# Stores of the weights' float32 words moved from SyncE's queue to GpSimd's, from the fifth block on

## The chip, the cores and the metric

The kernel runs on one core of a Trainium2 chip. The metric is the device time of one execution in microseconds (us). In the rows and in the text PE is TensorE, DVE is VectorE, ACT is ScalarE, POOL is GpSimd and SP is SyncE. SPq and POOLq are the instruction queues of SP and POOL, where DMAs are issued.

## The reference

Causal attention over 4 batches and 12 heads, then two dense layers with a gate from a short convolution, then a layer that rotates by an angle, mixes tokens and adds a dense layer. The inputs are float64; the kernel reads their bits and turns them into float32 itself.

```python
# attention: batch 4, heads 12, seq 448, head_dim 64  ->  x of (4, 448, 768)
attn = softmax(causal(q @ k.T / 8));  x = attn @ v
# dense 1: conv_w (5, 768), w_val and w_out (768, 768)
gate = sigmoid(sum_k conv_w[k] * shifted(x, k))
x = (gate * (x @ w_val)) @ w_out
# dense 2: w_theta, w_ch (768, 768), w_tok_r, w_tok_i (448, 448)
theta = x @ w_theta
y = w_tok_r @ (x * cos(theta)) + w_tok_i @ (x * sin(theta))
u = x + y
out = u + max(u @ w_ch, 0)
```

## The kernel before

Two streams are interleaved. `attention()` is a generator that does one head in five steps. `dense(b)` is a generator for the dense layers of one batch. The attention of batch b+1 is issued between the steps of `dense(b)`, at a pace set by the table `RATE`. A scheduler then fixes the order of each engine's instructions; the written order only guides it.

The weights come as four matrices of six blocks of 128 output columns: n = 0 to 5 is w_val, 6 to 11 is w_out, 12 to 17 is w_theta, 18 to 23 is w_ch. Each block has two halves, g = 0 and 1, of 384 rows. In the first batch a half goes through these steps:

- `load_w` (L202): SP issues the load of the float64 bits, 384 KB, into a tile `cv_raw`.
- `stage_w`, through `to_f32` (L156 to L163): three DVE instructions and one of ACT (L162) make float32 words of it, in place. L163 is the last.
- `split_w` (L221): for w_val and w_out, SP issues a store of these words, 192 KB, from `cv_raw` to a scratch tensor `plain` in HBM. Later batches load the words from there.
- `split_w` again: `pool_hi` (L107, POOL) rounds the words to the matmul's format, into a tile `w_hl`; `pool_lo` (L110, POOL) or `dve_lo` (L113, DVE) writes the remainder.
- `gemm` (L532): nine PE matmuls with the half.

`cv_raw` and `w_hl` share one pool of eight buffers, the tag `wb`. A load can start when the buffer that it gets is free: when POOL has read the old words and their store has landed, or when PE has used the old `w_hl`.

SP issues every DMA of the kernel, in order: loads of q, k, v and weights, the stores, the outputs. POOL issues none. Besides the weights, POOL computes the low parts of activations (`act_lo`, `x_lo`), a part of the convolution (`gate`, L480) and some copies of k (`kk`, L107).

Three more names: `rb` are the reciprocal row sums of the softmax, fetched by SP from a scratch tensor (L451); `z` are the angle's cosine and sine parts (L587 to L603, on ACT, DVE and POOL); L613 are PE's transposes of z, which the token mixing (L627) needs.

Of the kernel before, what the change touches and what calls it, by code (L numbers as in the profile page):

```python
# [33 lines left out]
AHEAD = 2  # L34
# [17 lines left out]
def kernel(  # L52
# [14 lines left out]
    nc = tc.nc  # L67
# [31 lines left out]
    def f32(ap):  # L99
        return ap.bitcast(F32)  # L100
# [5 lines left out]
    def pool_hi(dst, src):  # L106
        nc.gpsimd.tensor_scalar(out=dst, in0=src, scalar1=1.0, scalar2=0.0, op0=ALU.mult, op1=ALU.add)  # L107
# [82 lines left out]
    plain = dram.tile([NW, 2, P, KH * P], F32, name="plain")  # L190
# [3 lines left out]
    def words(t):  # L194
        return t.rearrange("p n two -> p (n two)")[:, 0:CV]
# [18 lines left out]
    def split_w(n, g):  # L214
        if (n, g) not in bits:
            return
        flat = words(bits.pop((n, g))).bitcast(F32)
        t = flat.rearrange("p (c n) -> p c n", n=P)
        kept = n % NW // KC in PLAIN
        if B > 1 and kept and n < NW:  # L220
            nc.sync.dma_start(out=plain[n, g], in_=flat)  # L221
        store = B > 1 and (kept and B > 2 if n >= NW else not kept)
        if n < AHEAD:
            hi, lo = (
                pool.tile([P, S], F32R, tag=tag, name="w_ahead", bufs=12)[:, : KH * P].rearrange("p (c n) -> p c n", n=P)
                for tag in ("act_hi", "act_lo")
            )
        else:
            hl = pool.tile([P, 2, KH, P], F32R, tag="wb", name="w_hl", bufs=8)
            hi, lo = hl[:, 0], hl[:, 1]  # L230
        if n < NW:
            pool_hi(hi, t)
        else:
            nc.scalar.copy(hi, t)  # L234
        (dve_lo if n < NW and int(W_DVE[n // KC]) > g else pool_lo)(lo, t, hi)
        if store and n < AHEAD:
            for a, x in enumerate((hi, lo)):
                nc.sync.dma_start(
                    out=scratch[n, g][:, a * KH * P : (a + 1) * KH * P], in_=f32(x.rearrange("p c n -> p (c n)"))
                )  # L240
        elif store:
            nc.sync.dma_start(out=scratch[n % NW, g], in_=f32(hl.rearrange("p a c n -> p (a c n)")))
        splits[n, g] = (hi, lo)
# [275 lines left out]
    def gemm(acts):  # L519
        n = wn[0]  # L520
        wn[0] += 1
        pt = psum("mm")
        for g in range(2):
            split_w(n + 1, g)
            stage_w(n + 2, g)
            load_w(n + 3, g)
            fetch_w(n + 3, g)
            whi, wlo = splits.pop((n, g))
            for kc in range(g * KH, (g + 1) * KH):
                xhi, xlo = acts[kc]  # L530
                for m, (a, x) in enumerate(((whi, xhi), (whi, xlo), (wlo, xhi))):
                    nc.tensor.matmul(  # L532
                        pt[:, :S], lhsT=a[:, kc % KH, :], rhs=x,
                        start=kc == 0 and m == 0, stop=kc == KC - 1 and m == 2,
                    )
            if g == 0:
                yield
        return pt
# [189 lines left out]
    for n in range(5 * (H + 1) + X_SEG + 1):  # L728
        next(at, None)
        if n == 5:  # L730
            setup_conv()
        if W_AT <= n < 5 * H:
            with tc.issue_after(ttr_ins[-1].ins):
                for at_n, (m, g) in zip(A_TILES, ((0, 0), (1, 0), (0, 1), (1, 1), (2, 0), (2, 1), (3, 0), (3, 1))):
                    if n == at_n - W_AT:
                        load_w(m, g)
                    if n == at_n:
                        stage_w(m, g)
                        if m < AHEAD + 1:
                            split_w(m, g)  # L740
        i, c = divmod(n, 5)
        if AHEAD and i >= 3 and i % 2 == 1 and c == A_SEG:
            gemm_ahead((i - 3) // 2)
        if n == 5 * H - 3:
            with tc.issue_after(ttr_ins[-1].ins):
                for g in range(2):
                    load_w(AHEAD + 2, g)
# [47 lines left out]
```

## Time and profile before

| | before |
|---|---|
| median of 3 runs (lowest to highest) | 778.81 us (778.42 to 780.77) |
| profiled execution, its own time | 784.47 us |
| its span, first to last instruction | 782.4 us |
| PE, DVE, ACT, POOL busy | 714.7, 463.3, 445.0, 331.9 us |
| stores to `plain` from SP | 24, of 192 KB |

The profiled execution has 2.07 us outside its span and is 5.66 us (0.7%) above the median. The shares of busy time are means over stages with different limits: the first batch's dense layers, about 100 to 260 us, are the only stage in which weights are converted and stored to `plain`.

### The profile page before, as it was taken

To read this page: it belongs to the slowest core of one execution; us is meant where nothing else is said; L and a number is where in the kernel's file an instruction comes from. 1 tells how busy PE (TensorE), PEld (TensorE's weight loads), DVE (VectorE), ACT (ScalarE), POOL (GpSimd) and SP (SyncE) were. 2 spreads that over 40 slices of the span, in tenths; PEclk is the share of its full clock that TensorE was granted. 3 is DMA by queue.
4 is the path that set the end of the run, shared out by engine and by line. 5 is a ranking of instruction groups with operands and counts; after the bars stand their busy time and mean duration, and the time that the engine had idled before them with its cause. 6 is when DMAs were issued, how large, how long until landed. Compare 5 with 4: busy or idle time off the path is not lost.

```text
span 782.4 us, 12216 instructions
## 1 busy us (share of the span) xinstructions
PE 714.7 (91%) x4009; PEld 607.5 (78%) x4009; DVE 463.3 (59%) x1104; ACT 445.0 (57%) x1047; POOL 331.9 (42%) x363
## 2 busy tenths in 40 slices
PE   5898978994988998999899999999899998999997
PEld 4665666783867886888688798898788887898996
DVE  4888599887777564463575564564576432115531
ACT  4787665876797454565877344354878331125401
POOL 0597774975476566774164410033062241201100
PEclk9999889998999999899999999999999999999999
DMA  9845337988684398799843288688532187774223
GB/s 227 181 122 146 78 106 224 208 265 187 193 143 123 103 208 279 233 224 338 152 75 99 54 171 232 193 141 240 143 61 66 52 135 233 203 220 139 84 71 81
DMA packets 152940, 125.78 MB, mean 161 GB/s; under 512 B 92815, under 2 KB 130477, under 8 KB 152877
## 3 DMA queue, kind: packets, MB, share of 16 engines
q1 hardware_dynamic: 152877, 125.00, 62.9%
q8 instruction: 32, 0.52, 0.3%
q14 instruction: 31, 0.25, 0.1%
HBM read 95.81 MB, written 29.16 MB: 160 GB/s over the span
## 4 chain that ended last, share of the span: by engine, by line
PE 58%; DVE 15%; ACT 10%; DMA 9%; issue 4%; POOL 2%; SPq 2%; DVEq 0%; ACTq 0%; POOLq 0%
PE ps_mm L532 31%; PE ps_mm L627 11%; PE ps_av L402 5%; PE ps_tr L379 3%; ACT prob L118 2%; DMA cv_raw<-in_moe_w_theta_dram 2%; PE ps_s L358 2%; PE ps_s L359 2%; DVE qs L113 2%; DMA scratch<-w_hl 2%; DVE ps_s L360 2%; DVE gate L494 2%; DVE klo L113 1%; DMA out_dram<-o 1%; DVE ps_cv L156 1%
## 5 line engine op out<-in xcount | busy, mean ns | idle before, releaser
L532 PE MATMUL ps_mm<-act_hi,w_hl 128*128 128x448 f32 x864 | 267.5, 372 | 1.4 <-DVE w_hl L113 0.7
L532 PEld LDWEIGHTS ps_mm<-act_hi,w_hl 128*128 128x128 f32 x864 | 161.7, 190 | 14.7 <-DVE w_hl L113 1.1
L532 PE MATMUL ps_mm<-act_lo,w_hl 128*128 128x448 f32 x432 | 157.9, 367 | 0.0
L360 DVE CUSTOM_DVE_ANT_0 ps_s<-ps_s,mask 112x112 f32<-112x112 f32 x192 | 85.9, 455 | 66.9 <-PE ps_s L359 53.8
L118 ACT ACTIVATE prob<-ps_s,negm 112x112 f32<-112x112 f32 x192 | 95.2, 497 | 50.6 <-DVE negm L360 49.3
L110 POOL TENSOR_TENSOR act_lo<-x2f,act_hi 128x448 fp32r<-128x448 f32 x36 | 42.8, 1188 | 109.8 <-DVE act_hi L544 52.2
L392 ACT COPY pt<-ps_tr 112x448 f32<-112x448 f32 (+3 forms) x132 | 53.6, 425 | 61.6 <-PE ps_tr L379 61.2
L379 PE MATMUL ps_tr<-ident,prob 112*112 112x112 f32 x480 | 78.4, 271 | 10.6 <-ACT prob L118 4.0
L532 PE MATMUL ps_mm<-x_hi,w_hl 128*128 128x448 f32 x264 | 83.4, 386 | 5.0 <-ACT x_hi L467 2.2
L532 PEld LDWEIGHTS ps_mm<-act_lo,w_hl 128*128 128x128 f32 x432 | 81.7, 190 | 5.0
L358 PE MATMUL ps_s<-kk,qs 128*112 128x256 f32 x192 | 71.7, 377 | 9.4 <-POOL kk L107 3.2
L379 PEld LDWEIGHTS ps_tr<-ident,prob 112*112 112x112 f32 x480 | 56.5, 137 | 24.8 <-ACT prob L118 7.0
L110 POOL TENSOR_TENSOR w_hl<-cv_raw,w_hl 128x384 fp32r<-128x384 f32 x62 | 64.5, 1042 | 13.5 <-ACT w_hl L234 10.9
L627 PE MATMUL ps_mm<-wtok_h,zt_h 128*128 128x448 f32 x168 | 63.8, 380 | 4.3 <-ACT zt_h L618 4.1
L627 PE MATMUL ps_mm<-wtok_h,zt_l 128*128 128x448 f32 x168 | 63.1, 375 | 0.6 <-DVE zt_l L113 0.5
L359 PE MATMUL ps_s<-klo,qs 128*112 128x256 f32 x192 | 62.0, 329 | 1.5 <-DVE klo L113 1.5
L627 PE MATMUL ps_mm<-wtok_l,zt_h 128*128 128x448 f32 x168 | 61.7, 367 | 0.0
L532 PEld LDWEIGHTS ps_mm<-x_hi,w_hl 128*128 128x128 f32 x264 | 51.7, 198 | 12.1 <-ACT x_hi L467 2.9
L603 POOL TENSOR_TENSOR z<-z,x2f 128x448 f32<-128x448 f32 x18 | 20.7, 1148 | 93.5 <-ACT z L600 93.5
L402 PE MATMUL ps_av<-pt,v_raw 112*64 112x448 f32 (+3 forms) x384 | 59.3, 430 | 0.5 <-ACT prob L118 0.5
L490 POOL TENSOR_TENSOR gate<-gate,tp 128x448 f32<-128x448 f32 x48 | 57.5, 1198 | 2.4
L110 POOL TENSOR_TENSOR x_lo<-xf,x_hi 128x448 fp32r<-128x448 f32 x23 | 27.9, 1213 | 61.1 <-ACT x_hi L467 60.5
(108 smaller groups left out, 1352.8 us busy)
## 6 DMA issues: line engine op xcount, KB each, us to landing
w_hl<-scratch SPq DMA_DIRECT2D x120, 384.0 KB, 3.8
scratch<-w_hl SPq DMA_DIRECT2D x48, 384.0 KB, 4.2
q_raw<-in_q_dram SPq DMA_DIRECT2D x48, 112.0 KB, 3.6
v_raw<-in_v_dram SPq DMA_DIRECT2D x24, 224.0 KB, 4.2
out_dram<-o SPq DMA_DIRECT2D x24, 224.0 KB, 3.3
cv_raw<-in_moe_w_val_dram SPq DMA_DIRECT2D x12, 384.0 KB, 5.3
plain<-cv_raw SPq DMA_DIRECT2D x24, 192.0 KB, 3.8
cv_raw<-in_moe_w_out_dram SPq DMA_DIRECT2D x12, 384.0 KB, 4.6
```

The lines of the kernel that those rows point to most:

```text
L110: nc.gpsimd.tensor_tensor(out=dst, in0=src, in1=f32(hi), op=ALU.subtract)
L113: return nc.vector.tensor_tensor(out=dst, in0=src, in1=f32(hi), op=ALU.subtract)
L118: exps.append(nc.scalar.activation(*args, **kw))
L358: nc.tensor.matmul(pt[:CP, :nn], lhsT=qs[:, cs], rhs=kk[:, :nn], start=True, stop=False)
L359: nc.tensor.matmul(pt[:CP, :nn], lhsT=qs[:, cs], rhs=klo[:, :nn], start=False, stop=True)
L360: ttr = nc.vector.tensor_tensor_reduce(out=pt[:CP, :n], in0=pt[:CP, :n], in1=mask[:, S - n : S], scale=-1.0 / math.sqrt(D), scalar=3.0e38, ...
L379: nc.tensor.transpose(pt[:CP, off : off + CP], prob[i, c][:, kc * CP : (kc + 1) * CP], ident[:CP, :CP])
L392: nc.scalar.copy(t, src)
L402: nc.tensor.matmul(av[g][j * D : (j + 1) * D, kc * CP : S], lhsT=tv[:, j, kc, :], rhs=pT.pop((2 * g + j, kc)), start=kc == 0, stop=kc == N ...
L490: nc.gpsimd.tensor_tensor(out=gt, in0=gt, in1=tp, op=ALU.add)
L532: nc.tensor.matmul(pt[:, :S], lhsT=a[:, kc % KH, :], rhs=x, start=kc == 0 and m == 0, stop=kc == KC - 1 and m == 2,)
L627: nc.tensor.matmul(pt[:, :S], lhsT=a[:, m, :], rhs=w[:, m, :], start=m == 0 and n == 0, stop=m == NZ - 1 and n == 2,)
```

## The change

Of the 24 stores to `plain` the first eight (n = 0 to 3) stay on SP. The other 16 (n = 4 and 5 of w_val, all of w_out) are issued by POOL. What is stored, and from where, stays the same.

```diff
         kept = n % NW // KC in PLAIN
         if B > 1 and kept and n < NW:
-            nc.sync.dma_start(out=plain[n, g], in_=flat)
+            (nc.sync if n < AHEAD + 2 else nc.gpsimd).dma_start(out=plain[n, g], in_=flat)
         store = B > 1 and (kept and B > 2 if n >= NW else not kept)
```

`AHEAD` is 2. The scheduler orders all engines anew with it. In the pieces below the number behind a tile's name tells tiles of one name apart, and what stands in brackets are the semaphores that the instruction waits on: `DVE`, `PE`, `Pool` and `Activation` count instructions of these engines, `DMAHW` DMAs that SP issued, `DMASW` DMAs that POOL issued.

POOL before, in the middle of w_out: the halves 1584 (n = 7) to 1666 (n = 8).

```order
L107 TENSOR_SCALAR w_hl_1730<-cv_raw_1584 128x384 [waits DMAHW4_49,DMAHW0_49,DVE_49]
L110 TENSOR_TENSOR w_hl_1730<-cv_raw_1584,w_hl_1730 128x384 [waits Pool_49]
L110 TENSOR_TENSOR act_lo_1793<-x2f_1790,act_hi_1792 128x448 [waits Activation_49]
L107 TENSOR_SCALAR w_hl_1771<-cv_raw_1610 128x384 [waits DMAHW6_49,DMAHW5_49,DVE_49]
L110 TENSOR_TENSOR w_hl_1771<-cv_raw_1610,w_hl_1771 128x384 [waits Pool_49]
L107 TENSOR_SCALAR w_hl_1868<-cv_raw_1666 128x384 [waits DMAHW1_49,DMAHW7_49,DVE_49,Activation_49]
```

POOL after the change, the same halves:

```order
L221 DMA plain_77<-cv_raw_1584 128x384 [waits DMAHW1_49,DVE_49,Activation_49]
L107 TENSOR_SCALAR w_hl_1730<-cv_raw_1584 128x384 [waits DMASW4_49]
L221 DMA plain_77<-cv_raw_1610 128x384 [waits DMAHW2_49,DVE_49]
L110 TENSOR_TENSOR w_hl_1730<-cv_raw_1584,w_hl_1730 128x384 [waits Pool_49]
L107 TENSOR_SCALAR w_hl_1771<-cv_raw_1610 128x384 [waits DMASW5_49]
L110 TENSOR_TENSOR act_lo_1793<-x2f_1790,act_hi_1792 128x448 [waits Activation_49]
L221 DMA plain_77<-cv_raw_1666 128x384 [waits DMAHW4_49,DVE_49]
L107 TENSOR_SCALAR w_hl_1868<-cv_raw_1666 128x384 [waits DMASW6_49,DMASW1_49,Pool_49]
```

Each store now stands ahead of its half's L107 in POOL's order, and L107 waits for an earlier store that POOL issued, whose buffer it writes.

SP before, the end of w_out's loads and the first of w_theta:

```order
L221 DMA plain_77<-cv_raw_1876 128x384 [waits DMAHW0_49,DVE_49]
L202 DMA cv_raw_2037<-in_moe2_w_theta_dram 128x3x256 [waits DMAHW6_49,DMAHW1_49,Pool_49]
L221 DMA plain_77<-cv_raw_1903 128x384 [waits DMAHW2_49,DVE_49]
L202 DMA cv_raw_2070<-in_moe2_w_theta_dram 128x3x256 [waits DMAHW3_49,PE_49]
L221 DMA plain_77<-cv_raw_1950 128x384 [waits DMAHW5_49,DMAHW4_49,DVE_49]
L202 DMA cv_raw_2111<-in_moe2_w_theta_dram 128x3x256 [waits DMAHW2_49,Pool_49]
L298 DMA v_raw_2096<-in_v_dram 112x8x64 [waits PE_49]
L451 DMA rb_2098<-rows_1844 64x448 [waits DMAHW7_49]
```

SP after the change, the same loads:

```order
L298 DMA v_raw_2096<-in_v_dram 112x8x64 [waits DMAHW4_49,PE_49]
L451 DMA rb_2098<-rows_1844 64x448 [waits DMAHW5_49,DMAHW0_49]
L451 DMA rb_2098<-rows_1844 64x448 [waits DMAHW6_49]
L202 DMA cv_raw_2037<-in_moe2_w_theta_dram 128x3x256 [waits DMASW0_49,PE_49,DMAHW7_49,Activation_49,Pool_49]
L202 DMA cv_raw_2070<-in_moe2_w_theta_dram 128x3x256 [waits DVE_49,DMASW4_49,Activation_49,Pool_49]
L202 DMA cv_raw_2111<-in_moe2_w_theta_dram 128x3x256 [waits DMAHW1_49,DMASW2_49,PE_49]
```

The stores are gone from between the loads; the loads wait for stores of POOL (`DMASW`) instead, and stand behind the load of v and the two loads of `rb` that stood behind them.

## Rows read from the trace of the kernel before

**Rows 1.** The page: span, busy time of each engine, and POOL in 40 slices

```profile
span 782.4 us, 12216 instructions
...
PE 714.7 (91%) x4009; PEld 607.5 (78%) x4009; DVE 463.3 (59%) x1104; ACT 445.0 (57%) x1047; POOL 331.9 (42%) x363
...
POOL 0597774975476566774164410033062241201100
```

**Rows 2.** Busy time by stretch (columns in the first row)

```profile
core 0: us, PE busy (x) PEld busy (x) DVE busy (x) ACT busy (x) POOL busy (x), PEclk, DMA share, GB/s
...
112.00:129.50 17.50, 14.78 (x65) 11.28 (x64) 16.98 (x39) 9.71 (x23) 7.14 (x8) 0.80 0.74 234
129.50:165.40 35.90, 33.65 (x194) 28.04 (x195) 31.61 (x73) 26.52 (x67) 29.92 (x36) 0.95 0.90 221
165.40:185.40 20.00, 18.37 (x102) 16.03 (x100) 17.43 (x39) 15.20 (x39) 15.96 (x18) 1.00 0.98 246
185.40:194.90 9.50, 0.33 (x2) 0.00 (x1) 6.88 (x17) 5.97 (x10) 2.42 (x4) 0.64 0.68 174
...
260.00:782.00 522.00, 497.48 (x2795) 436.47 (x2793) 261.08 (x604) 259.76 (x582) 165.98 (x168) 0.99 0.62 158
```

**Rows 3.** POOL's groups, 129.5 to 165.4 us: count | busy, mean ns | idle before

```profile
L110 POOL TENSOR_TENSOR w_hl<-cv_raw,w_hl 128x384 fp32r<-128x384 f32 x12 | 12.1, 1016 | 0.7
L107 POOL TENSOR_SCALAR w_hl<-cv_raw 128x384 fp32r<-128x384 f32 x13 | 6.9, 537 | 9.6 <-ACT act_hi L548 4.9 <-DVE cv_raw L163 3.5 <-DMA plain<-cv_raw 1.1
L110 POOL TENSOR_TENSOR act_lo<-x2f,act_hi 128x448 fp32r<-128x448 f32 x4 | 4.6, 1154 | 0.3 <-ACT act_hi L546 0.3
L480 POOL TENSOR_TENSOR gate<-gate,tp 128x448 f32<-128x448 f32 x4 | 4.6, 1140 | 0.0
L110 POOL TENSOR_TENSOR x_lo<-xf,x_hi 128x448 fp32r<-128x448 f32 x1 | 1.2, 1159 | 0.0
L107 POOL TENSOR_SCALAR kk<-kk 64x448 fp32r<-64x448 f32 x2 | 1.1, 561 | 0.2
```

**Rows 4.** Waits of SP's queue from 112 to 166 us: total, times, longest

```profile
SPq L221 <- DVE cv_raw L163: 15.4, 11, 3.8
SPq L202 <- DMA plain<-cv_raw: 8.4, 3, 3.8
```

**Rows 5.** The stores to plain from 112 to 164 us: issue (ns) and landing

```profile
L221 SPq DMA_DIRECT2D plain<-cv_raw x16: 326/340/1382, 112.5 to 163.1; - x16
...
DMA to landing us min/median/max: 2.6/4.0/8.8
```

**Rows 6.** DVE's groups from 129.5 to 165.4 us: the first step of the conversion

```profile
L156 DVE TENSOR_SCALAR ps_cv<-cv_raw 128x384 int32<-128x384 uint32 x12 | 6.6, 554 | 3.3 <-DMA cv_raw<-in_moe_w_out_dram 1.7 <-DMA cv_raw<-in_moe_w_theta_dram 1.3 <-ACT pt L392 0.4
```

**Rows 7.** DVE's waits from 165.4 to 200 us

```profile
DVE ps_cv L156 <- DMA cv_raw<-in_moe_w_theta_dram: 5.0, 5, 3.6
```

**Rows 8.** PE's waits from 112 to 200 us

```profile
PE ps_tr L613 <- DVE z L602: 9.2, 1, 9.2
...
PE ps_mm L532 <- POOL w_hl L110: 0.8, 2, 0.4
```

**Rows 9.** The timeline around PE's longest wait

```profile
178.04 0.39 SPq L202 DMA_DIRECT2D cv_raw<-in_moe_w_theta_dram  x1
...
188.02 0.56 DVE L156 TENSOR_SCALAR ps_cv<-cv_raw 128x384 int32<-128x384 uint32 x1 [3.62 <-DMA cv_raw<-in_moe_w_theta_dram]
...
189.26 0.39 DVE L591 TENSOR_SCALAR z<-z 128x448 int32<-128x448 int32 x1
...
191.75 0.58 ACT L600 ACTIVATE z<-z 128x448 f32<-128x448 f32 x1
...
194.17 0.61 DVE L602 TENSOR_TENSOR z<-z,x2f 128x448 f32<-128x448 f32 x1
```

**Rows 10.** L107 on weight words over the whole span: ns, min/median/max

```profile
L107 POOL TENSOR_SCALAR w_hl<-cv_raw x44: 507/513/1266, 54.4 to 292.3; 128x384 fp32r<-128x384 f32 x44
```

## The prediction

> **What bounds the kernel now.** The page comes first: PE is busy 91% of the span, POOL only 42% [rows 1]. By that share POOL has room for anything. But POOL's slices run from 0 to 9, so the mean says nothing about the place of the change. I therefore asked for the busy time by stretch [rows 2]. From 260 us on, PE is busy 497.48 of 522 us, and none of the changed stores lies there, so what happens before goes through to the end unless a gap of PE swallows it. The 16 stores that move are issued between 112.5 and 163.1 us [rows 5]: four in the stretch from 112 to 129.5 us (n = 4 and 5), the twelve of w_out after it. In the first stretch DVE is busy 16.98 of 17.5 us: DVE is the limit there, and POOL, with 7.14, is far from one. From 129.5 to 165.4 us four resources are close together: PE 33.65, DVE 31.61 and POOL 29.92 of 35.9 us, and the DMA engines at 0.90. POOL has 35.9 - 29.92 = 5.98 us left. From 165.4 to 185.4 us PE is busy 18.37 of 20 us and the DMA engines 0.98. Then PE does nothing for 9.5 us [rows 2].
>
> PE's waits name that gap: 9.2 us, once, for z [rows 8]. The timeline tells why z is late [rows 9]. DVE works in order, and the first step of a weight's conversion (L156) stood ahead of the next step of z (L591). L156 waited 3.62 us for a load of w_theta, issued at 178.04 us, some 9.98 us before L156 could start at 188.02. So of the gap 3.6 us are a late load, and the rest is z's own chain.
>
> **What it removes.** SP's queue spent 15.4 us waiting for DVE ahead of the stores, and 8.4 us ahead of loads whose buffer a store still read [rows 4]. The 15.4 go, with 16 issues of 0.34 us (5.4 us); the 8.4 do not, since the loads now wait for the same landings under another name. SP's time is worth nothing by itself. What it can give is earlier loads, and what these can give is the time that DVE waited for them: 1.7 + 1.3 = 3.0 us from 129.5 to 165.4 us [rows 6], 5.0 us after it [rows 7]. Together 8.0 us is the most that the removal can return.
>
> **What it adds.** POOL issues 16 DMAs in order with its own work. Each stands ahead of the half's L107, and POOL's store delays that half's L107 and L110, the next store, and everything behind. No row of before shows a DMA issued by POOL, so its price S is bounded by the nearest rows. Below: SP's issue of the same store, 0.34 us [rows 5]. Above: POOL's longest instruction on such a half, L107's 1.27 us [rows 10]; its usual ones are 0.51 (L107) and 1.02 us (L110) [rows 3, 10]. I take S = 1.0, like L110: SP is there only to issue, whereas POOL needs over half a microsecond even for the simplest pass over a half, and a store also goes to each of its 128 partitions. The Trainium skill, "DMA: Bandwidth & Descriptors" (section "Latency and other measured facts"), says that a DMA issued by GpSimd has its descriptors written by software there, with the first byte after about 1 us, against some 0.6 us from SyncE; no row here shows it, and the estimate by that figure alone would put 12 x 1.0 = 12 us on POOL in w_out's stretch.
>
> - First stretch, four stores: 4 x 1.0 = 4.0 us into 17.5 - 7.14 = 10.4 us of POOL's idle time. Two of them stand ahead of the first half's L110, for which PE already waits (0.8 us in two waits [rows 8]), so PE may start a block 2.0 us late. PE is idle 17.5 - 14.78 = 2.7 us there, and DVE, the limit, has other work. I cost it at 0; without that cover it is 2.0 us.
> - w_out's stretch, twelve stores: 12 x 1.0 = 12.0 us into 5.98 us. POOL becomes the limit: 12.0 - 5.98 = +6.0 us. The bounds: at S = 0.34 it is 4.1 us, all hidden, 0; at S = 1.27 it is 15.2 - 5.98 = +9.3 us. The point at which POOL starts to decide is S = 5.98 / 12 = 0.50 us.
> - The new waits: L107 writes a buffer whose store POOL itself issued, about five instructions earlier (see the POOL piece: 1610's L107 waits for a store two halves back). Those halves are about 5 us of POOL's work (two stores, 2.0; two L107, 1.0; two L110, 2.0). The stores took 4.0 us in the median to land, 8.8 at most [rows 5]. In the median this is covered; a landing of 8.8 us would cost 3.8 us, and as the same wait cost 1.1 us in all before [rows 3], I add nothing and keep 3.8 for the range.
>
> **What that gives back.** While POOL is the limit, DVE's 3.0 us of waits inside w_out's stretch [rows 6] lie beside POOL's excess and return nothing. Behind it there are 5.0 us [rows 7]: 3.6 in PE's gap and 1.4 elsewhere. With w_out's stretch 6.0 us longer, the same bytes have more time, so the DMA engines (0.98 busy from 165.4 to 185.4 us [rows 2]) should jam less and the load of 178.04 us land sooner. Against it: the new order puts w_theta's first loads behind the load of v and two of `rb`. I take the middle between 1.4 and 5.0: -3.2 us. DVE's and ACT's orders change, but no instruction is added or lost on them, nor an ACT table load: 0. The sum is +6.0 - 3.2 = **+2.8 us**. The profiled execution would go from 784.47 to 787.3 us. It is 5.66 us above the median; the difference is carried over to the median: 778.81 + 2.8 = **781.6 us**.
>
> **Rivals.**
>
> 1. *Cheap issues: faster.* If POOL only hands the store on, S is near SP's 0.34 us, POOL stays under its 5.98 us, and SP no longer stops its loads. Then DVE's 5.0 us behind w_out [rows 7] go, since the loads run ahead, and 3.0 more at most [rows 6]: 778.81 - 5.0 = 773.8, and 770.8 at the extreme. For it: SP waits 15.4 us ahead of these stores [rows 4]. Against it: loads still need a free buffer, and DVE is busy 31.61 of 35.9 us [rows 2], so early loads wait for DVE. It decides below S = 0.50.
> 2. *Nothing moves.* DVE's limit up to 129.5 us hides the first four stores, and PE's 9.2 us gap [rows 8] swallows the 6.0 us of the rest, since its work ahead of the gap is done early anyway: z waits for the loads, not for PE. Time 778.8. Against it: z and these loads come behind w_out's halves on POOL and DVE, so the gap is pushed along with them.
> 3. *POOL is held up.* POOL's instructions on a half are at times stretched: L107 took 1.27 us at most against 0.51 in the median [rows 10], 0.75 us more. If each of twelve stores met that, 12 x 0.75 = 9.0 us would be added to the 2.8: 778.81 + 11.8 = 790.6. Against it: from 129.5 to 165.4 us L107 has a mean of 0.537 us [rows 3], so it is rare there. The Trainium skill, "SBUF — State Buffer" (section "SBUF: two separate sides"), has a rule for this: while DVE runs certain instructions GpSimd is locked out of a port that they share, cannot write descriptors, and its DMA stalls until DVE ends. By that rule rival 3 holds; the mean of 0.537 us speaks for few such meetings in this stretch.
>
> **How the numbers follow.** 0.3% of the median, 2.3 us, is about what a measurement of this kernel tells from no change. POOL as the limit, by the sum above: 0.43, with 779 to 785 us for itself (S from 0.75 to 1.25, which is +3.0 to +9.0, less 3.2). Cheap issues: 0.22. Nothing moves: 0.21. Held up: 0.14. Slower holds all of the last and 0.30 of the first: 0.44. Faster holds rival 1 but for 0.01, and the luck of a new order on all engines, 0.04: 0.25. The rest is same: 0.31. The range goes from rival 1's 773.8 to 789, short of rival 3's full price; about 0.1 is left out at either side.
>
> **What would show it.** S directly: the profile after should have 16 stores on POOL's queue, and POOL's groups from 129 us on show idle time or gaps of S each. POOL's busy time and those gaps should fill w_out's stretch, which should be about 6 us longer than 35.9. PE should wait for `w_hl` from POOL (L107, L110) far more than 0.8 us there. The stores should be gone from SP's waits, and its waits for a landing remain. PE's gap before L613 should be 3 us shorter than 9.2. The prediction is wrong if S is under 0.5 us, if w_out's stretch is not longer, or if the gap of PE takes up its lengthening.

## The result and the profile after

The changed kernel takes 791.99 us in the median of four runs (789.72 to 794.05), against 779.79 us for the kernel before beside it. The ratio of the runs is put at 1.0119 (95% interval 1.0079 to 1.0159), below that of the two medians, which stand 12.2 us apart, and the text goes by it: slower by 9.3 us (779.79 x 0.0119). The forecast of 781.6 us had the sign right and the size far too small: the time lies outside its range, which ended at 789. The profiled execution has a span of 791.3 us, 8.9 more than before.

Busy time by stretch, with the columns and the cuts of [rows 2] (the last row begins at 270 us, not 260):

```profile
112.00:129.50 17.50, 15.66 (x73) 12.56 (x72) 16.65 (x39) 9.10 (x23) 9.66 (x14) 0.80 0.77 241
129.50:165.40 35.90, 27.69 (x153) 21.92 (x152) 27.89 (x61) 22.31 (x56) 27.04 (x36) 0.90 0.61 167
165.40:185.40 20.00, 16.96 (x80) 14.96 (x79) 13.36 (x30) 11.48 (x30) 13.23 (x17) 0.83 0.55 175
...
270.00:791.30 521.30, 497.86 (x2790) 436.38 (x2789) 260.45 (x602) 259.16 (x580) 165.33 (x168) 0.98 0.62 159
```

From 270 us on the kernel is the old one: 521.3 us, where the one before needed 522 from 260. The loss lies ahead of that. It is not that POOL is full: from 129.5 to 165.4 us POOL is busy 27.04 of 35.9 us, its issues counted, less than before, and so are PE (27.69 against 33.65), DVE (27.89 against 31.61) and the DMA engines (0.61 against 0.90). Everybody waits. POOL itself stands idle for 8.2 us ahead of the ten stores in this window (count | busy, mean ns | idle before):

```profile
L221 POOL DMA_DIRECT2D plain<-cv_raw x10 | 5.8, 580 | 8.2 <-ACT wtok_h L185 4.0 <-DVE cv_raw L163 2.2 <-issue 2.0
```

The window is one of the clock, and it holds less of the work than before: POOL does 8 of its L107 on weights in it, against 13 in [rows 3]. Measured by the work, w_out's stretch did get longer. From ACT's conversion of w_val's last output (L548) to its copy of w_out's last (L579) it is 40.8 us before and 55.6 after (ACT's timeline, before and then after):

```profile
129.05 0.56 ACT L548 CAST act_hi<-hf 128x448 fp32r<-128x448 f32 x1 [0.36 <-DVE hf L570]
...
169.81 0.52 ACT L579 ACTIVATE x2f<-ps_mm 128x448 f32<-128x448 f32 x1
```

```profile
128.06 0.57 ACT L548 CAST act_hi<-hf 128x448 fp32r<-128x448 f32 x1
...
183.69 0.52 ACT L579 ACTIVATE x2f<-ps_mm 128x448 f32<-128x448 f32 x1
```

That length is not the price by itself, for PE's order is a new one too: in the run below that has SP's queue alone in the old order it is 52.2 us, at a ratio of 1.0015. The price of a store on POOL, L221 on POOL over the whole span (ns, min/median/max), and its landing:

```profile
L221 POOL DMA_DIRECT2D plain<-cv_raw x16: 539/587/752, 109.6 to 163.1; - x16
...
DMA to landing us min/median/max: 2.2/3.5/8.8
```

0.587 us, not 1.0. Now the waits. DVE from 129 to 200 us, then SP's queue from 140 to 166 us (total, times, longest):

```profile
DVE ps_cv L156 <- DMA cv_raw<-in_moe_w_theta_dram: 9.9, 2, 5.1
DVE ps_cv L156 <- DMA cv_raw<-in_moe_w_out_dram: 4.7, 1, 4.7
```

```profile
SPq L298 <- PE ps_av L402: 8.5, 1, 8.5
SPq L202 <- PE ps_mm L532: 7.3, 1, 7.3
SPq L425 <- DVE rec L418: 2.9, 1, 2.9
```

DVE waits 14.6 us for loads of weights, against 3.0 + 5.0 before [rows 6, 7]. The 15.4 us that SP waited for DVE at the stores [rows 4] are gone, and it waits for PE and DVE at other rows. Its waits for the landing of a store fell from 8.4 us [rows 4] to 2.7 (SP's queue from 112 to 166 us):

```profile
SPq L202 <- DMA plain<-cv_raw: 2.7, 1, 2.7
```

SP's timeline from 138 to 166 us shows the other rows:

```profile
138.39 0.37 SPq L202 DMA_DIRECT2D cv_raw<-in_moe_w_out_dram  x1
138.86 1.02 SPq L290 DMA_DIRECT2D q_raw<-in_q_dram  x2
139.97 0.97 SPq L290 DMA_DIRECT2D k_raw<-in_k_dram  x2
143.87 0.31 SPq L425 DMA_DIRECT2D rows<-rec  x1
144.36 8.77 SPq L202 DMA_DIRECT2D cv_raw<-in_moe_w_out_dram  x3
161.71 0.33 SPq L298 DMA_DIRECT2D v_raw<-in_v_dram  x1
162.14 1.25 SPq L451 DMA_DIRECT2D rb<-rows  x2
163.58 2.63 SPq L202 DMA_DIRECT2D cv_raw<-in_moe_w_theta_dram  x2
```

With the stores gone the scheduler put SP's other transfers in a new order. Two places stand out. The tenth load of w_out stood ahead of the loads of k and of the store `rows<-rec` before; now it stands behind them. And the loads of w_theta stand behind the load of v, at which SP waits 8.5 us for PE's attention. PE's gap before L613, 9.2 us before [rows 8], is 10.4; for the halves of POOL, `w_hl`, PE waits 1.8 us, against 0.8 (PE's waits from 112 to 215 us):

```profile
PE ps_tr L613 <- DVE z L602: 10.4, 1, 10.4
...
PE ps_mm L532 <- POOL w_hl L110: 1.8, 2, 1.4
```

One thing more. `rows<-rec` is 3.5 KB, the smallest transfer in this timeline. The DMA engines in steps of 2 us around it (columns as in [rows 2]; the last two are their busy share and GB/s), and what was issued from 143 to 146 us (KB each, median us to landing):

```profile
142.00:144.00 2.00, 1.48 (x8) 1.03 (x6) 1.94 (x6) 1.62 (x4) 1.89 (x3) 1.00 0.85 222
144.00:146.00 2.00, 0.13 (x1) 0.14 (x2) 2.00 (x5) 1.93 (x4) 0.56 (x1) 1.00 0.29 14
146.00:148.00 2.00, 2.00 (x12) 1.89 (x12) 1.94 (x5) 1.21 (x3) 1.35 (x3) 0.59 0.33 22
148.00:150.00 2.00, 2.00 (x10) 1.50 (x8) 1.15 (x2) 0.79 (x2) 2.00 (x3) 0.56 0.47 36
150.00:152.00 2.00, 1.44 (x10) 1.36 (x10) 0.00 (x0) 0.53 (x2) 1.88 (x3) 1.00 0.43 38
152.00:154.00 2.00, 0.62 (x4) 0.23 (x2) 0.07 (x1) 0.00 (x0) 1.64 (x3) 1.00 0.89 292
```

```profile
cv_raw<-in_moe_w_out_dram SPq DMA_DIRECT2D x2, 384.0 KB, 9.9
rows<-rec SPq DMA_DIRECT2D x1, 3.5 KB, 7.0
```

For 8 us next to nothing moves (14 to 38 GB/s), and the loads behind the store take 9.9 us. In the kernel before, the same tenth load was issued at 142.29 us, ahead of the store, and took 5.1 us; the next load, behind it, took 9.0, and there too the engines moved only 13 GB/s from 148 to 150 us (the kernel before, issued from 143 to 146 us and from 146 to 148 us):

```profile
rows<-rec SPq DMA_DIRECT2D x1, 3.5 KB, 9.9
...
cv_raw<-in_moe_w_out_dram SPq DMA_DIRECT2D x1, 384.0 KB, 9.0
```

PE's clock (the column PEclk, where 1.00 is the upper of its two levels, 2.4 GHz, and 0.50 the lower, 1.2 GHz) shows such waits too. From 144 to 146 us PE was busy for 0.13 us, and then the granted clock was 0.59 and 0.56 up to 150 us, most of that time at the lower level. Over the whole span PE is busy 717.0 us with its 4009 matmuls, 2.3 more than before [rows 1]: a small part of the loss.

### The profile page after: what moved, and what is told of

Its sections match the earlier page's. It is cut to its first block, busy times and chain, and to the rows that moved or that the text cites. A ratio compares the mean times of both kernels' runs of the same rounds, so it can differ in the third digit from the quotient of the medians.

```text
span 791.3 us, 12222 instructions
## 1 busy us (share of the span) xinstructions
PE 717.0 (91%) x4009; PEld 609.2 (77%) x4009; DVE 468.1 (59%) x1104; ACT 444.5 (56%) x1047; POOL 340.8 (43%) x379
## 4 chain that ended last, share of the span: by engine, by line
PE 60%; DVE 15%; ACT 10%; DMA 7%; issue 4%; POOL 2%; SPq 1%; DVEq 0%; POOLq 0%; ACTq 0%
PE ps_mm L532 32%; PE ps_mm L627 11%; PE ps_av L402 5%; PE ps_tr L379 3%; ACT prob L118 2%; PE ps_s L358 2%; PE ps_s L359 2%; DMA cv_raw<-in_moe_w_theta_dram 2%; DVE qs L113 2%; DVE gate L494 2%; DVE klo L113 1%; PE ps_tr L613 1%; DVE ps_cv L159 1%; DVE ps_cv L156 1%; ACT L600 1%
## 5 line engine op out<-in xcount | busy, mean ns | idle before, releaser
L110 POOL TENSOR_TENSOR act_lo<-x2f,act_hi 128x448 fp32r<-128x448 f32 x36 | 42.8, 1189 | 109.6 <-DVE act_hi L544 53.8
L110 POOL TENSOR_TENSOR w_hl<-cv_raw,w_hl 128x384 fp32r<-128x384 f32 x62 | 64.0, 1035 | 15.3 <-ACT w_hl L234 13.4
L110 POOL TENSOR_TENSOR x_lo<-xf,x_hi 128x448 fp32r<-128x448 f32 x23 | 27.8, 1208 | 61.4 <-ACT x_hi L467 61.0
```

What stands on the lines that cost most here:

```text
L110: nc.gpsimd.tensor_tensor(out=dst, in0=src, in1=f32(hi), op=ALU.subtract)
```

## The experiments

Three theories. *Order*: the loss comes from the new order, above all SP's. *POOL*: POOL's issues, or stores that leave later because POOL comes to them later, cost it. And, from the trace above, *scatter*: it is what `rows<-rec` does to the loads behind it. Orders are held by chaining each instruction of an engine to the one that stands ahead of it in a table, without a semaphore:

```python
tc.add_manual_dep(ins, prev.name, mybir.DependencyInfo(NoSync, DATA), reason="order")
```

Each ratio is to runs of the kernel before on the same chip, with its 95% interval.

**Whose order, whose queue.** Four runs. The first two exchange order and queue:

```diff
 # e1: PE, DVE, ACT, SP, POOL in the order of before
-nc.sync.dma_start(out=plain[n, g], in_=flat)
+(nc.sync if n < AHEAD + 2 else nc.gpsimd).dma_start(out=plain[n, g], in_=flat)
 # e2: the source of before (all stores on SP); every engine in the order of the changed kernel
```

> The 16 stores are issued on POOL as in the change, each straight ahead of its half's L107; all else on every engine keeps the order of the kernel before (PE, DVE and ACT row for row, SP without the 16 stores). Theory 'order' (the loss of 12.2 us comes from the new order that the scheduler made: DVE starves for loads that stand behind other transfers on SP's queue, and PE takes attention and turns of tokens ahead of weights): the ratio to before is 1.000, between 0.993 and 1.004. Theory 'POOL' (what the prediction held: the issues and the waits for landings on POOL cost it): 1.008 to 1.016, as in the change, and PE waits for w_hl from POOL for several us.

Measured 1.0056 (1.0023 to 1.0089): about half the loss, between the two theories. Here PE does wait for POOL's halves, 4.6 us in all (PE's waits from 112 to 215 us):

```profile
PE ps_mm L532 <- POOL w_hl L110: 2.4, 4, 1.1
PE ps_mm L532 <- POOL w_hl L107: 2.2, 4, 1.1
```

> The 16 stores are issued on SP's queue as before the change, but every engine keeps the order that the changed kernel had (PE, DVE and ACT row for row, POOL without the stores, SP with the stores put in at the places of the time at which POOL issued them). Theory 'order': the loss stays, ratio 1.008 to 1.016. Theory 'POOL': it goes, ratio 0.997 to 1.004.

Measured 1.0172 (1.0120 to 1.0224). With no store on POOL the loss is all there: the order costs it. The stores on SP, in an order made without them, make it worse rather than better.

The changed kernel with SP's queue alone held (the scheduler is free to move the rest):

> The changed kernel with SP's queue alone held in the order of the kernel before (without the stores); the other engines are ordered freely by the scheduler. Theory 'order', in the form that SP's queue is what starves DVE: the ratio comes down to 1.000 to 1.005. In the form that PE's order (attention and turns of tokens ahead of weights) costs it: it stays at 1.008 to 1.016 as far as that order stays. Theory 'POOL': 1.008 to 1.016.

Measured 1.0056 (1.0024 to 1.0089): about half of the loss is given back, but other engines moved too. And the issues of the first run doubled:

```diff
+for r in (0, P // 2):
+    nc.gpsimd.dma_start(out=plain[n, g, r : r + P // 2], in_=flat[r : r + P // 2])
```

> As the run with every engine in the order before and the stores on POOL, but each store is cut into two of 64 partitions, so POOL issues 32 DMAs for the same bytes. Theory 'order': within 0.3% of that run (POOL's issues are hidden, some 0.4 to 0.6 us each). Theory 'POOL': another 5 to 9 us on top of that run, a ratio near 1.02.

Measured 1.0101 (1.0043 to 1.0159): 0.45% above the first run, 3.5 us for 16 more issues of 0.553 us in the median, 8.8 us in all. The intervals overlap. Both theories missed: the issues are neither free nor paid in full.

**POOL's issue, and when the store leaves.** First the issue alone, then the store behind its half's split:

```diff
 # e5: the kernel before, in its order
+if n >= AHEAD + 2:
+    nc.gpsimd.dma_start(out=plain[n + 2 * KC, g][:, 0:16], in_=ident[:, 0:16])
```

> The kernel before, its order kept on every engine and its stores left on SP, but POOL issues 16 extra small DMAs (128 partitions of 64 bytes, from a constant tile to memory that nobody reads), one straight ahead of the L107 of each of the 16 halves: POOL's issue time alone, with no store later than before. The run with the stores on POOL in the order before cost 0.56%. Theory 'issue time' (some 0.6 us of POOL each, 12 of them where POOL has 5.98 us left): the same loss, a ratio from 1.003 to 1.009. Theory 'late stores' (POOL issues a store only when it comes to that half, so that the buffer comes free later and SP's load waits for the landing): 0.998 to 1.002.

Measured 1.0023 (0.9993 to 1.0053), between the theories and not told from zero. An issue of 8 KB holds POOL as long as one of 192 KB (ns, min/median/max):

```profile
L223 POOL DMA_DIRECT2D plain<-ident x16: 586/586/750, 108.0 to 164.2; - x16
```

```diff
 # e6: order of before; on POOL, for each of the 16 halves
-L221 DMA plain<-cv_raw
 L107 TENSOR_SCALAR w_hl<-cv_raw
 L110 TENSOR_TENSOR w_hl<-cv_raw,w_hl
+L221 DMA plain<-cv_raw
```

> As the run with the stores on POOL in the order before, but each store stands behind its half's L110 instead of ahead of its L107, some 1.5 us later; POOL's sum of work is the same, and the half is split 0.6 us earlier. Theory 'issue time': as that run or better, a ratio from 1.000 to 1.006. Theory 'late stores': worse than that run, 1.008 to 1.015, with longer waits of SP's loads for landings.

Measured 0.9991 (0.9959 to 1.0022). Late stores show no cost in this order. A store ahead of the split that PE waits for does (1.0056), by the two intervals only just, for one ends at 1.0022 and the other begins at 1.0023. In the old order POOL's part is thus 0.2 to 0.9% with the stores placed as in the change.

**SP's queue alone.** Every other engine is held, so only SP's rows move:

```diff
 # e7: PE, DVE, ACT, POOL as in the changed kernel; SP as before. e8: the converse
 L202 DMA cv_raw<-in_moe_w_out_dram        # the ninth
 L290 DMA q_raw<-in_q_dram x2
+L202 DMA cv_raw<-in_moe_w_out_dram        # the tenth
 L290 DMA k_raw<-in_k_dram x2
 L425 DMA rows<-rec
-L202 DMA cv_raw<-in_moe_w_out_dram
 L202 DMA cv_raw<-in_moe_w_out_dram x2
-L298 DMA v_raw<-in_v_dram
-L451 DMA rb<-rows x2
 L202 DMA cv_raw<-in_moe_w_theta_dram x3
+L298 DMA v_raw<-in_v_dram
+L451 DMA rb<-rows x2
...
```

(Behind these rows are a few more swaps of the kind, two loads of w_theta and the third store of rows among them.)

> The changed kernel with the order of PE, DVE, ACT and POOL that it had, row for row, and SP's queue alone in the order of before (loads of w_out and w_theta ahead of v, rb and rows where they stood so before). Theory 'SP's order' costs the half of the loss that the stores on POOL in the old order do not: the ratio comes down to 1.003 to 1.008. Theory 'PE's order' (attention and token turns taken ahead of weights): it stays at 1.010 to 1.015.

> The converse: the stores on POOL, every engine in the order of before, and SP's queue alone in the order that the changed kernel had. Theory 'SP's order': 1.010 to 1.016, as the changed kernel. Theory 'PE's order': 1.003 to 1.008, as with the order of before everywhere.

Measured 1.0015 (0.9981 to 1.0049) and 1.0141 (1.0099 to 1.0182). This is the clearest pair: SP's old order takes the loss away while the stores stay on POOL and PE keeps its new order, and SP's new order brings it with PE in the old one, where the stores on POOL alone gave 1.0056. Neither pair of intervals overlaps (1.0015 and the change's 1.0119; 1.0141 and 1.0056). In the second run SP stands at the load of v for 14.8 us (its waits from 140 to 166 us), with the loads of w_theta behind it:

```profile
SPq L298 <- PE ps_av L402: 14.8, 1, 14.8
```

**Which rows.** I took the load of v to be it.

> The changed kernel with every engine's order as it had it, but for three rows of SP: the load of v and the two loads of rb stand behind the first three loads of w_theta (as before the change) instead of ahead of them. Theory 'three rows' (SP waits at the load of v for PE's attention while the loads of w_theta, whose buffers are free, stand behind it): most of the loss goes, a ratio from 0.999 to 1.006. Rival 'other rows of SP's order' (rows and k ahead of the tenth load of w_out, and later swaps): 1.009 to 1.015.

Measured 1.0114 (1.0070 to 1.0158): that theory fell. The other place:

> The changed kernel in its own order, but for one row of SP: the load of w_out that stood ahead of the loads of k and the store of rows before the change stands ahead of them again. Theory 'three rows': the loss stays, 1.008 to 1.015. Rival 'other rows of SP's order': down to 1.000 to 1.006.

Measured 1.0061 (1.0026 to 1.0096): one load, moved ahead of k and `rows`, gives back about half. DVE's wait for w_out, 4.7 us in the changed kernel, is 2.7 (its waits from 129 to 200 us):

```profile
DVE ps_cv L156 <- DMA cv_raw<-in_moe_w_out_dram: 2.7, 2, 2.2
```

The three rows (v, rb, rb) in the kernel before, ahead of w_theta's loads:

> The kernel before, with its stores on SP and its order on every engine, but for the three rows: the load of v and the two of rb stand ahead of the first load of w_theta, as in the changed kernel. Theory 'three rows': the loss appears with no store moved, a ratio from 1.008 to 1.018. Rival 'other rows', or a loss that needs the stores on POOL: 0.998 to 1.004.

Measured 1.0067 (1.0036 to 1.0098): under the expected 1.008, yet a loss. In that order the place of v costs; in the changed kernel's it gives nothing back. And the two best edits together:

> The changed kernel with SP's queue in the order of before, and with POOL's store of each half behind its L110 instead of ahead of its L107; PE, DVE and ACT in the order of the changed kernel. If the two edits add up (SP's order alone gave 1.0015, the store behind the split took 0.6% off in the order of before): 0.994 to 0.998. If the place of the store only matters in the order of before: 0.999 to 1.004.

Measured 1.0080 (1.0047 to 1.0114), above both expectations and above the 1.0015 without the move of the stores. They do not add up: in this order the late store does hold SP's loads (its waits from 112 to 215 us; 3.1 us in the run without the move).

```profile
SPq L202 <- DMA plain<-cv_raw: 21.2, 7, 6.3
```

**The scattered store.** `rows<-rec` writes a 112x8 tile, turned, as 896 words of 4 bytes. One of the stores in longer runs, with every engine's order as it was. The words of its two heads then stand in another order, so these kernels leave out the right scale of two heads:

```diff
-nc.sync.dma_start(out=rows.rearrange("h c p -> p h c"), in_=rec)
+if g == NP + 1:
+    line = rows.rearrange("h c p -> (h c p)")
+    nc.sync.dma_start(out=line.rearrange("(p x) -> p x", x=2 * NC), in_=rec.rearrange("p h c -> p (h c)"))
+else:
+    nc.sync.dma_start(out=rows.rearrange("h c p -> p h c"), in_=rec)
```

> The changed kernel, every engine in its order, but for one transfer: the second store of rows (3.5 KB, issued on SP at 143.87 us in the changed kernel, 896 single words of 4 bytes scattered in memory) is written as 112 runs of 32 bytes instead, so that the words of these two heads stand in another order (the scale of their rows is then wrong). Theory 'scatter' (from 144 to 152 us the DMA engines moved 14 to 38 GB/s while that store landed, in 7.0 us; the load of w_out that the new order put behind it took 9.9 us, where one ahead of it takes 3.6 to 4.6): the store lands in 2 to 4 us, the load in 4 to 6, and a ratio from 1.000 to 1.007. Rival 'place alone' (SP waits in order for PE and for buffers, whatever that store costs): 1.009 to 1.015.

> The same one transfer in the kernel before, every engine in its order: what the scatter costs there, where two loads of w_out stand behind it (9.0 and 8.8 us to land). Theory 'scatter': it costs there too, but less, since the load that DVE needs next is ahead of it: a ratio from 0.993 to 0.999. Rival 'place alone': 0.998 to 1.002.

Measured 1.0068 (1.0041 to 1.0096) and 0.9953 (0.9925 to 0.9981). One store of 3.5 KB costs about 0.5% in either kernel, clear of zero before the change; in the changed kernel the intervals with and without it still overlap a little. The kernel before with that store in longer runs: what was issued from 143.4 to 144.9 us, and the DMA engines from 144 to 150 us (its store is issued at 143.19 us):

```profile
cv_raw<-in_moe_w_out_dram SPq DMA_DIRECT2D x1, 384.0 KB, 3.4
...
rows<-rec SPq DMA_DIRECT2D x1, 3.5 KB, 3.5
```

```profile
144.00:146.00 2.00, 1.43 (x10) 1.08 (x8) 1.94 (x5) 1.95 (x4) 1.91 (x3) 1.00 0.90 220
146.00:148.00 2.00, 1.82 (x11) 1.20 (x11) 1.97 (x6) 1.95 (x5) 1.92 (x4) 1.00 0.94 282
148.00:150.00 2.00, 1.19 (x6) 0.92 (x6) 1.95 (x6) 2.00 (x6) 1.83 (x3) 1.00 0.69 199
```

The engines no longer stop, and the store lands in 3.5 us instead of 9.9. But as both kernels gain about as much, this store does not explain the difference between them: 1.0068 / 0.9953 is still 1.0116. Then all 18 stores, with nothing left out; the scheduler is free to order both kernels anew:

```diff
+pt = psum("tr")
+nc.tensor.transpose(pt[: 2 * NC, :CP], rec.rearrange("p h c -> p (h c)"), ident[:CP, :CP])
+turned = pool.tile([2 * NC, CP], F32, tag="rec_t", name="turned")
+nc.scalar.copy(turned, pt[: 2 * NC, :CP])
-nc.sync.dma_start(out=rows.rearrange("h c p -> p h c"), in_=rec)
+nc.sync.dma_start(out=rows.rearrange("h c p -> (h c) p"), in_=turned)
```

> The kernel before with all 18 stores of rows written as 8 runs of 448 bytes: PE turns the 112x8 tile rec into 8x112 first and ACT copies it out. All of it is computed as before. Theory 'scatter': the stores land in 2 to 4 us instead of 8.6, the DMA engines do not stop, and the ratio is 0.985 to 0.998; most of that before 260 us, since PE is busy 95% behind it. Rival 'place alone', or the scheduler's new order taking it back: 0.998 to 1.006.

> The changed kernel with the same edit of all 18 stores. If the change loses its time by what the scatter does to the loads behind it, it loses little here: within 0.5% of the run before with that edit. If POOL's issues or the place in SP's queue cost it: 0.8 to 1.4% more than that run.

Measured 0.9958 (0.9932 to 0.9983) and 1.0043 (1.0016 to 1.0069). The first is faster than the kernel before, by 3.3 us. DVE's and PE's waits in it, from 112 to 215 us, one line each, against 6.2 us for w_theta in the same window of the kernel before and PE's 9.2:

```profile
DVE ps_cv L156 <- DMA cv_raw<-in_moe_w_theta_dram: 3.1, 2, 2.7
```

```profile
PE ps_tr L617 <- DVE z L606: 5.3, 1, 5.3
```

The change still costs 0.85% on top of it (1.0043 / 0.9958). *Scatter* alone is out as its cause.

**What is left.** Long runs and the place of v at once, and then the buffers: the scheduler deals the eight buffers of the weights anew with each order, so a load waits for another tile's last reader. (The runs above with moved rows may hold a new deal too; they do not tell place and deal apart.)

> The changed kernel in its own order with two edits at once: the one store of rows (the second) in 32-byte runs as before (so that two heads' scale is wrong), and the load of v and the two of rb behind the first three loads of w_theta. Each edit alone gave 1.0068 and 1.0114. Theory 'two causes' (a load of w_out behind the scattered store, and the loads of w_theta behind the wait for v; the second shows only once the first is gone): the loss goes, a ratio from 0.995 to 1.003. Rival 'something else' (POOL's issues, PE's order, or the buffers that the scheduler dealt): 1.004 to 1.010.

Measured 1.0066 (1.0037 to 1.0095): no better than long runs alone. The place of v is out as the cause in the changed kernel.

The deal alone, the same edit at every tile of the pool:

```diff
-t = pool.tile([P, CV, 2], I32, tag="wb", name="cv_raw", bufs=8)
+t = pool.tile([P, CV, 2], I32, tag=f"wb{next(deal)}", name="cv_raw", bufs=1)
```

> The kernel before, every engine in its order and the stores on SP, but each tile of the weights' eight buffers in the buffer that it had in the changed kernel (another deal of the same eight, from the tenth load of w_out on). Theory 'order of SP's queue': 0.998 to 1.003. Rival 'deal' (each load waits for another buffer's last reader, whatever the order): 1.005 to 1.012.

Measured 1.0057 (1.0020 to 1.0093): the changed kernel's deal costs the kernel before half a per cent, with not one instruction moved.

## Why the prediction was wrong

- **S was mis-sized.** Taken at 1.0 us, between 0.34 and 1.27; measured 0.587. It lies above the 0.50 at which POOL was to decide, so by the prediction's own sum w_out's stretch should have grown by 12 x 0.587 - 5.98 = 1.1 us, not 6.0. With the -3.2 us of the give-back that sum is -2.1 us, a faster kernel: that the forecast had the sign right was luck.
- **"POOL becomes the limit" failed.** POOL has 8.9 us left from 129.5 to 165.4 us and waits itself. That w_out's stretch grew by 14.9 us, a sign named for it, came of other waits: PE's for `w_hl` from POOL are 1.8 us. Rival 3 (POOL held up) failed as well: the longest issue took 0.752 us, and that its 790.6 us is the nearest number to the measured one is luck too. The rule of the Trainium skill, "SBUF — State Buffer" (section "SBUF: two separate sides"), which bore on it is seen in no issue here. The Trainium skill, "DMA: Bandwidth & Descriptors" (section "Latency and other measured facts"), gives a first byte after about 1 us for such a DMA; no row here shows a first byte. What the rows show is the landing: 3.5 us in the median for the stores on POOL, no later than the 4.0 of those on SP [rows 5].
- **The step that failed is the give-back.** It was put at -3.2 us, with the remark that the new order puts w_theta's first loads behind v and two of `rb`, and that remark got no term of its own, only a part in the choice of the middle. DVE's waits for loads did not fall by 3.2 us but grew by 6.6 (14.6 against 8.0), and PE's gap grew to 10.4 us. A new order of SP's queue was a mechanism with a place and a price, and should have been a rival. The prediction also named the wrong rows in it: the tenth load of w_out behind `rows<-rec` was in the difference of the two orders, and is not named there.
- **What stands in its place.** Shown: SP's new order, with the deal of buffers that came with it, makes the loss (1.0015 without it, 1.0141 with it and the other engines in the old order, against 1.0056 for the stores on POOL there). Likely, since 1.0061 and the change's 1.0119 have intervals that just overlap: half of it is the one load of w_out behind the loads of k and the store `rows<-rec`. Open: the other half. Where it lies can be read in the traces: at w_theta's loads. With the second store in longer runs DVE's wait for w_out is 0.2 us, but its waits for w_theta are 10.9, and with the tenth load moved they are 9.4; with SP's old order they are 6.8, and before they were 6.2 (two of these lines stand below). What makes them is not settled. The place of v is excluded by two runs. The deal is able to cost as much (1.0057 in the old order). Two loads of w_theta that the changed kernel has behind the third store of `rows` take 10.8 us to land, and DVE waits 5.1 us for one; with SP's old order no wait for w_theta is longer than 3.4. Against this store as the whole of it: with all 18 stores in long runs, and an order of its own, the change still costs 0.85%, and DVE's waits for w_theta are 9.2 us against 3.1. Neither the deal nor the place of these two loads was tried alone in the changed kernel.

DVE's waits from 112 to 215 us, the changed kernel with the second store in longer runs and then with SP's queue alone in the old order:

```profile
DVE ps_cv L156 <- DMA cv_raw<-in_moe_w_theta_dram: 10.9, 3, 5.8
```

```profile
DVE ps_cv L156 <- DMA cv_raw<-in_moe_w_theta_dram: 6.8, 3, 3.4
```

DVE's timeline of the changed kernel, and its transfers issued from 183 to 190 us (KB each, median us to landing):

```profile
199.22 0.56 DVE L156 TENSOR_SCALAR ps_cv<-cv_raw 128x384 int32<-128x384 uint32 x1 [5.09 <-DMA cv_raw<-in_moe_w_theta_dram]
```

```profile
cv_raw<-in_moe_w_theta_dram SPq DMA_DIRECT2D x2, 384.0 KB, 10.8
...
rows<-rec SPq DMA_DIRECT2D x1, 3.5 KB, 10.9
```

PE's gap is no measure of the loss. It is 5.3 us with SP's queue alone in the old order (PE's waits from 112 to 215 us), but 10.7 in the kernel before with the second store in longer runs, at 0.9953:

```profile
PE ps_tr L613 <- DVE z L602: 5.3, 1, 5.3
```

- **The other rivals.** Rival 1 (cheap issues) had S under 0.50, and rival 2 (nothing moves) had PE's gap swallow a later w_out: 0.587 us and the loss itself spoke against both.
- **What held.** The stores left SP's waits, the first four cost nothing visible (ACT's conversion of w_val's last output comes at 128.06 us, at 129.05 before), and behind 270 us the kernel is the old one. SP's waits for landings, which were to stay at 8.4 us, fell to 2.7.

That the order of before with the stores on POOL lost 0.56%, with 4.6 us of PE's waits for POOL's halves, and nothing that the runs tell once each store stood behind its half's split, is the only part of the loss that resembles the mechanism forecast: a store delays the L107 and L110 behind it.

## What to carry to other kernels

Where a scheduler orders the queues, a transfer that is taken off a queue can change the order of all that remain there, and the deal of their buffers with it, as here; look through the new order of that queue row by row, and ask of each load what now stands ahead of it and what that waits for. To learn whether an effect is the edit's or the order's, hold every engine in the old order, then one engine at a time. And look at the smallest transfers too: here the price of one was in what landed behind it.

## What the runs showed that was not expected

A store of 3.5 KB in 896 words of 4 bytes took 7.0 to 10.9 us to land in the rows above, and in the changed kernel the second of them all but stopped the DMA engines for 8 us (14 to 38 GB/s). Loads behind it on its queue landed late (9.9 us), and so did a store on POOL's own queue (8.8 us, issued from 146 to 148 us). In 112 runs of 32 bytes, in the kernel before, it landed in 3.5 us and the engines kept 199 to 282 GB/s. The Trainium skill, "DMA: Bandwidth & Descriptors" (section "Rules for kernel authors"), has the rule that a transfer whose last dimension is not contiguous becomes one descriptor per element and should be rearranged. The trace agrees: with that one store in 112 runs an execution has 152156 packets against 152940, which is 896 - 112 = 784 fewer. The store may also bear on the forecast's reading of PE's gap: the load of w_theta that was 9.98 us on its way [rows 9] was issued half a microsecond ahead of such a store. No run tried that store alone.

```profile
178.52 0.53 SPq L425 DMA_DIRECT2D rows<-rec  x1
```

That row of the kernel before stood in its timeline from the start.

The issue of a DMA holds POOL for 0.55 to 0.59 us, whether it moves 8, 96 or 192 KB.
